# The end of a long convolution rewritten: tables closed two ticks sooner, a w_in block in a kernel tile's free half, the last units in a written order

## The chip, the cores and the metric

The program runs on one core of one Trainium2 chip. Its time is the device time of one execution in microseconds (us). Before and after are compared by the median of their runs. The engines are PE (TensorE matmul, with PEld for its weight loads), DVE (VectorE), ACT (ScalarE), POOL (GpSimd) and SP (SyncE, which here only issues DMAs).

## The reference

Two halves follow each other on a [2048, 576] activation. The first is a long convolution per channel (an S4 layer), whose kernel K is a sum of 128 complex exponentials; the second is a gated MLP with a spatial product over time.

```
h = layernorm(x) * (1 + ca) + sa
K = einsum("dn,dnl,dn->dl", C, exp(dt * A * l), dt * B).real       # 576 channels, 2048 taps
x = x + ga * (irfft(rfft(h) * rfft(K)) + h * Dskip)
h = layernorm(x) * (1 + cb) + sb
z = gelu(h @ w_in)                                                 # w_in [576, 4608]
z1, z2 = z[:, :2304], layernorm(z[:, 2304:])
x = x + gb * ((z1 * (w_sp @ z2 + b_sp)) @ w_out)
```

## The kernel before

`ssm` is the first half. It makes the taps from tables (exp, sin and cos on ScalarE, products on VectorE) in 36 groups `g` of 16 channels, and the convolution from small transforms on PE. All of it runs in *ticks* of one loop: in tick t the tables of group t are made, `kg_unit` multiplies those of group t-3, `k1_unit` transforms group t-4 and writes it into a k1 tile. The channels fall into five blocks `c` (four of 128, the last, `NC - 1`, of 64). For each block, units `i` follow: `u_load` and `u_unit` bring in and transform the input, `z_unit` multiplies it with the k1 tile, `v_unit` transforms back and writes rows to the DRAM tensor `v_d`. Then four y units `(c, q)`, each of four row tiles, read `v_d` back transposed (`y_vload`, two DMAs), add x (`y_xload`) and write `x1_d`. A dictionary `plan` holds the tick of each. A unit of 128 channels is written (c, q) below with c from 0, so (2, 0) to (4, 3) are the last twelve y units.

In the tick loop a scheduler may reorder the instructions. After the loop, `mlp.nc = mlp.tied` records the rest in program order on each engine (the helper's line 132 then stands for all of them in the profile), so what stands first in the code is issued first on its queue. That holds for the code after the loop and for `phase_a`.

SyncE issues the loads in its order. A DMA waits on its queue for the release of its buffer, for the data in DRAM that it reads, and for the landing of the DMA issued eight before it. POOL issues the writes in the same way.

The tables stand in a pool `tb`; `tabs.close()` gives its space to the second half: `mc`, `wzp` (with `wz`, the split w_in), `xz` and `stg` with two staging tiles `wst`. The second half of w_in (the z2 columns) comes in five blocks q of 512 columns (the last of 256). Each goes through four steps: `start_load` (three DMAs, 1.125 MB), `start_sum` (a sum of squares on ScalarE), `win_scale` (a product with ones on PE, then a power of two by small VectorE operations), `start_hi` (the fp16 high part, ScalarE) and `start_lo` (the low part and the last 64 rows, VectorE). Blocks 0 and 1 are loaded in ticks 20 and 24. Blocks 2 and 3 are loaded into `stg` after the loop, and block 4 in `phase_a`.

`phase_a` makes z2 for 16 row tiles `b`: statistics, `roots` and `ln2_rows` on VectorE, `turn` (five transposes on PE), the nt tile (high half by ScalarE in `turn_hi`, low half by VectorE in `turn_lo`), then five blocks of 14 matmuls `z2_mm(b, h)` against w_in block h, with a gelu each. A sum or scale recorded between two `z2_mm` stands between them on PE. `phase_b` is the spatial product and the output, and the change does not touch it.

PE's results of the convolution go through four PSUM buffers (`ps1`). The pools `xb`, `za`, `zb` and `v` have two buffers, `ue` and `us` four, `u1` five.

Of the kernel before, what the change touches and what calls it, by code (L numbers as in the profile page):

```python
# [144 lines left out]
def ssm(tc, I, x1_d, consts_s, dram, mod_d, mlp):  # L145
# [5 lines left out]
    with ExitStack() as ctx:  # L151
# [272 lines left out]
        def kg_unit(g):  # L424
# [8 lines left out]
            kk = kab[g] = tb.tile([128, 4, 64], F32, name="kab")  # L433
# [6 lines left out]
        def k1_unit(g):  # L440
            c, gi = divmod(g, 8)
            if gi == 0:
                k1t[c] = kp.tile([128, 32, 128], F32, name="k1")
            kk = kab.pop(g)
# [72 lines left out]
        def y_vload(c, q):  # L517
# [9 lines left out]
            if c == NC - 2 and q < 2:  # L527
                vt = [part("za"), part("zb")]
            else:
                vt = [part("u1", 5)[:, :4 * w] for _ in range(2)]  # L530
# [77 lines left out]
        for tick in range(NG + 4):  # L608
# [60 lines left out]
        tabs.close()  # L669
        mlp.nc = mlp.tied  # L670
        V, A, G, T, S = mlp.nc.vector, mlp.nc.scalar, mlp.nc.gpsimd, mlp.nc.tensor, mlp.nc.sync
        c3, c4 = NC - 2, NC - 1
        y_vload(2, 2)
        mlp.start()
        mlp.start_load(2)
        y_xload(2, 2)
        mlp.start_x1()
        for i in range(2):
            z_unit(c4, i)
            v_unit(c3, 6 + i)  # L680
        mlp.start_sum(0)
        for i in range(2):
            z_unit(c4, 2 + i)
            v_unit(c4, i)
            mlp.win_scale(5 + i, False)
            if i == 0:
                mlp.start_sum(1)
        mlp.start_hi(0)
        v_unit(c4, 2)
        v_unit(c4, 3)  # L690
        for c, r in ((2, 3), (c3, 0), (c3, 1), (c3, 2), (c3, 3), (c4, 0), (c4, 1), (c4, 2), (c4, 3)):
            y_xload(c, r)
        mlp.start_hi(1)
        mlp.start_lo(0)
        y_unit(2, 1)
        for c, r in ((2, 3), (c3, 0), (c3, 1), (c4, 0), (c4, 1)):
            y_vload(c, r)
        mlp.start_sums(ps2(), ps2())
        mlp.start_lo(1)
        y_unit(2, 2)  # L700
        y_vload(c3, 2)
        mlp.start_rows()
        mlp.start_sum(2)
        y_unit(2, 3)
# [57 lines left out]
class Mlp:  # L762
# [46 lines left out]
    def win_scale(self, q, inv=True):  # L809
        V, wcol = self.nc.vector, self.wcol  # L810
        self.total(wcol(q, N_W), q, 1)
# [4 lines left out]
    def win_last(self, q, t, dst):  # L816

        s = self.wcol(q, S_W)
        self.hi(dst[:, 8], t[:, 4], s)
        self.lo(dst[:64, 9], t[:64, 4], s[:64], dst[:64, 8])  # L820
# [65 lines left out]

    def start_sum(self, q):
# [730 lines left out]
```

## Time and profile before

| | us |
|---|---|
| median of 3 runs | 1798.19 (1791.86 to 1798.38) |
| profiled execution | 1798.62 |
| its span on the core | 1796.9 |
| PE busy | 1695.7 (94%) |
| DVE busy | 1128.8 (63%) |
| ACT busy | 785.6 (44%) |
| POOL busy | 224.0 (12%) |

The tick loop fills the first 400 us or so, `phase_a` runs from about 444 to 693, `phase_b` to the end. In the tables of windows each row has the busy time of the engines in a stretch, with the number of instructions, then the clock granted to PE, the mean share of time in which the 16 DMA engines worked (above 1 where transfers overlap on one engine), and GB/s. In timelines an entry has its start, its duration, engine, line, operation, tiles and shape, and in brackets the idle time of the engine ahead of it with what released it. SPq is SyncE's queue: the row is the issue of a DMA.

### The profile page before, as it was taken

How to read it: one execution, taken by the hardware profiler on the slowest of the kernel's cores; microseconds unless marked ns; L12 is line 12 of the kernel's file. 1: busy time of each engine (PE TensorE's matmuls, PEld its weight loads, DVE VectorE, ACT ScalarE, POOL GpSimd, SP SyncE). 2: the span in 40 equal slices, each digit the busy share in tenths (PEclk: the TensorE clock that was granted, in tenths of full speed). 3: DMA queues.
4: the chain of work that ended last, by engine and by line, in shares of the span. 5: the costliest groups of instructions: out<-in, count | busy, mean ns of one | idle time of the engine just before them, and what ended most of it. 6: DMA issues, size and time to landing. Idle time of an engine off the chain costs nothing.

```text
span 1796.9 us, 34078 instructions
## 1 busy us (share of the span) xinstructions
PE 1695.7 (94%) x14202; PEld 1197.6 (67%) x14202; DVE 1128.8 (63%) x2253; ACT 785.6 (44%) x1021; POOL 224.0 (12%) x350
## 2 busy tenths in 40 slices
PE   4687999996899999999999999999999999999999
PEld 1344555565455545877787777877778777887787
DVE  6987999857888997999784444474222265222322
ACT  4658999844476666555441322241111132011110
POOL 1321232342122211000000000000000000000000
PEclk8788999998899999999999999999999999999999
DMA  8457445779588788877564675562655472555520
GB/s 274 139 196 243 139 119 163 195 207 314 169 266 261 241 259 246 301 277 257 206 216 148 240 250 206 212 250 92 227 192 197 173 264 69 176 181 175 199 83 27
DMA packets 153034, 361.57 MB, mean 201 GB/s; under 512 B 24832, under 2 KB 68224, under 8 KB 150960
## 3 DMA queue, kind: packets, MB, share of 16 engines
q1 hardware_dynamic: 110272, 167.30, 29.4%
q0 software_dynamic: 33120, 153.95, 25.8%
q10 hardware_dynamic: 9488, 38.16, 5.3%
q8 instruction: 111, 1.82, 0.4%
q14 instruction: 43, 0.35, 0.1%
HBM read 256.86 MB, written 93.05 MB: 195 GB/s over the span
## 4 chain that ended last, share of the span: by engine, by line
PE 51%; DVE 16%; DMA 7%; issue 4%; ACT 4%; SPq 0%; POOL 0%; ACTq 0%; DVEq 0%; POOLq 0%
PE ps L1324 9%; PE ps L1359 8%; PE ps L1361 8%; PE ps L1360 8%; PE pz L132 3%; PE ps L1408 3%; PE ps L1409 3%; PE ps L1410 3%; DMA raw<-in_w_spT 2%; DVE zset L1066 2%; DVE gt L1373 2%; DMA z_d<-z 2%; ACT z L132 1%; DVE bsz L132 1%; PE pk L132 1%
## 5 line engine op out<-in xcount | busy, mean ns | idle before, releaser
L1359 PE MATMUL ps<-wsp,zset 128*128 128x256 f16 x2016 | 549.5, 273 | 2.8 <-DVE gt L1373 2.6
L1361 PE MATMUL ps<-wsp,zset 128*128 128x256 f16 x2016 | 549.5, 273 | 0.2 <-DVE zset L1066 0.2
L1360 PE MATMUL ps<-wsp,zset 128*128 128x256 f16 x2016 | 549.5, 273 | 0.0
L132 PE MATMUL pz<-wz,nt 128*128 128x512 f16 (+1 forms) x1120 | 227.2, 363 | 9.0 <-ACT nt L132 5.5
L1373 DVE SCALAR_TENSOR_TENSOR gt<-ps,sc,bsp 128x512 f32<-128x512 f32 x36 | 27.0, 749 | 316.1 <-PE ps L1361 316.1
L1324 PE MATMUL ps<-n2q,wf 128*128 128x512 f16 x1008 | 223.3, 379 | 0.6 <-DMA wf<-win_d 0.6
L1359 PEld LDWEIGHTS <-zset 128*128 128x128 f16 x2016 | 197.5, 98 | 29.7 <-DVE gt L1373 3.2
L1360 PEld LDWEIGHTS <-zset 128*128 128x128 f16 x2016 | 197.2, 98 | 26.1
L1361 PEld LDWEIGHTS <-zset 128*128 128x128 f16 x2016 | 197.3, 98 | 23.3 <-DVE zset L1066 0.5
L132 PEld LDWEIGHTS <-nt 128*128 128x128 f16 x1120 | 110.2, 100 | 117.4 <-ACT nt L132 7.2
L1324 PEld LDWEIGHTS <-wf 128*128 128x128 f16 x1008 | 98.6, 98 | 112.6 <-DMA wf<-win_d 1.1
L1336 POOL DMA_DIRECT2D zset<-set_d x96 | 51.1, 532 | 969.3 <-PE ps L1361 939.3
L1329 ACT ACTIVATE z<-ps,sc 128x512 f32<-128x512 f32 x56 | 37.8, 681 | 280.5 <-PE ps L1324 278.0
L1409 PE MATMUL ps<-wout,z 128*128 128x288 f16 x448 | 128.1, 286 | 0.0
L1408 PE MATMUL ps<-wout,z 128*128 128x288 f16 x448 | 128.1, 286 | 0.0
L1410 PE MATMUL ps<-wout,z 128*128 128x288 f16 x448 | 128.1, 286 | 0.0
L1373 DVE SCALAR_TENSOR_TENSOR gt<-ps,sc,gt 128x512 f32<-128x512 f32 (+1 forms) x180 | 121.9, 694 | 5.8 <-DVE gt L1373 0.5
L1066 DVE TENSOR_TENSOR zset<-raw,zset 128x1024 f16<-128x1024 f32 x48 | 58.6, 1220 | 74.7 <-ACT zset L1065 74.7
L1065 ACT ACTIVATE zset<-raw 128x1024 f16<-128x1024 f32 x48 | 50.3, 1051 | 97.5 <-PE ps L1361 70.1
L132 ACT ACTIVATE z<-pz,sc 128x512 f32<-128x512 f32 (+1 forms) x80 | 49.6, 646 | 56.8 <-DMA z_d<-z 44.4
L1418 DVE TENSOR_TENSOR ot<-ot,ps 128x288 f32<-128x288 f32 x32 | 14.2, 452 | 82.7 <-ACT ot L1417 82.7
L369 PE MATMUL ps<-ln_x,r1t 128*128 128x288 f32 x128 | 43.6, 499 | 19.0 <-issue 12.6
(311 smaller groups left out, 2827.5 us busy)
## 6 DMA issues: line engine op xcount, KB each, us to landing
zset<-set_d POOLq DMA_DIRECT2D x96, 896.0 KB, 4.9
set_d<-zset ACTq DMA_DIRECT2D x36, 896.0 KB, 5.8
raw<-z_d SPq DMA_DIRECT2D x48, 512.0 KB, 4.6
wf<-win_d SPq DMA_DIRECT2D x72, 320.0 KB, 3.4
raw<-in_w_spT SPq DMA_DIRECT2D x43, 512.0 KB, 6.0
z_d<-z POOLq DMA_DIRECT2D x32, 576.0 KB, 7.8
u_d<-st1o POOLq DMA_DIRECT2D x16, 576.0 KB, 4.5
u<-u_d SPq DMA_DIRECT2D x36, 256.0 KB, 4.8
```

What stands on the lines that cost most here:

```text
L132: return self.tc.keep_in_program_order(f(*a, **k))
L1065: nc.scalar.activation(o[:, k, 0], t, AF.Copy)
L1066: nc.vector.tensor_tensor(o[:, k, 1], t, o[:, k, 0], op=ALU.subtract)
L1324: nc.tensor.matmul(pm.rearrange("p (t c) -> p t c", t=4), w[:, kw], self.n2[q][:, :, kn], start=i == 0, stop=i == len(Z1) - 1)
L1336: self.nc.gpsimd.dma_start(o, self.set_d[n // 4, n % 4])
L1359: T.matmul(pm, z[:, a, 0, c], w[:, b, 0], start=i + half == 0, stop=False, skip_group_check=True)
L1360: T.matmul(pm, z[:, a, 0, c], w[:, b, 1], start=False, stop=False, skip_group_check=True)
L1361: T.matmul(pm, z[:, a, 1, c], w[:, b, 0], start=False, stop=i == 7, skip_group_check=True)
L1373: V.scalar_tensor_tensor(dst, pm, inv, to, op0=ALU.mult, op1=ALU.add)
L1408: T.matmul(pl, p[:, 1, ts], w[:, 0, hs], start=st, stop=sp)
L1409: T.matmul(pa, p[:, 0, ts], w[:, 0, hs], start=st, stop=False)
L1410: T.matmul(pa, p[:, 0, ts], w[:, 1, hs], start=False, stop=sp)
```

## The change

Seven things change together.

1. The tick loop ends two ticks sooner (`NG + 2`). What it would have recorded in ticks 38 and 39 is now written out after it, in program order, and between these units stand the first steps of the second half. `tabs.close()` comes after `kg_unit(NG - 1)` and `k1_unit(NG - 2)`, and the last group's `kab` tile lies in an `xb` buffer.
2. Block 2 of w_in is loaded in the tick loop into the half of the last k1 tile that 64 channels leave free (`load_two`, 1 MB), its last 64 rows later into a `u1` buffer (`load_last`). Its sum of squares is two instructions, added by one reduction (`sum_two`, `total(..., 20, 2)`).
3. `stg` takes blocks 3 and 4, so that `start_load(3)` stands ahead of most y loads, and `start_load(4)` behind them but ahead of `phase_a`.
4. The low parts of blocks 0 and 1 are written in two pieces each among the z and v units (`start_lo(q, 0)` and `start_lo(q, 1)`; the second is `last`, the two operations that `win_last` had).
5. Y unit (2, 1) stands between the v units of the last block; units (3, 0), (2, 2) and (4, 0) come first after them, then the normed rows of tile 0, then the other eight.
6. Sum, scale, high and low part of block 2, and sum, scale and high part of block 3 are ahead of `phase_a`. There `start_lo(3)` stands behind `turn_lo(0)`, and block 4's four steps around the first gelu.
7. Y load (2, 3) takes the `za` and `zb` buffers that (3, 0) had; (3, 0) takes `u1`.

The core of the diff:

```diff
-            kk = kab[g] = tb.tile([128, 4, 64], F32, name="kab")
+            if g < NG - 1:
+                kk = kab[g] = tb.tile([128, 4, 64], F32, name="kab")
+            else:
+                kk = kab[g] = part("xb")[:, :256].rearrange("p (i w) -> p i w", i=4)
...
+                if c == NC - 1:
+                    t = k1t[c].rearrange("p a b -> p (a b)")
+                    k1t[c] = t[:, :32 * CHL].rearrange("p (a b) -> p a b", b=CHL)
+                    mlp.load_two(2, t[:, 32 * CHL:].rearrange("p (k n) -> p k n", k=4))
...
-            if c == NC - 2 and q < 2:
+            if (c, q) in ((NC - 2, 1), (NC - 3, 3)):
                 vt = [part("za"), part("zb")]
...
-        for tick in range(NG + 4):
+        for tick in range(NG + 2):
...
-        tabs.close()
         mlp.nc = mlp.tied
         V, A, G, T, S = mlp.nc.vector, mlp.nc.scalar, mlp.nc.gpsimd, mlp.nc.tensor, mlp.nc.sync
-        c3, c4 = NC - 2, NC - 1
-        y_vload(2, 2)
+        c2, c3, c4 = NC - 3, NC - 2, NC - 1
+        y_load(c2, 0)
+        u_load(c4, 2)
+        u_load(c4, 3)
+        z_unit(c3, 4)
+        z_unit(c3, 5)
+        v_unit(c3, 2)
+        v_unit(c3, 3)
+        kg_unit(NG - 1)
+        d_unit(NG - 1)
+        u_unit(c4, 0)
+        u_unit(c4, 1)
+        k1_unit(NG - 2)
+        tabs.close()
         mlp.start()
-        mlp.start_load(2)
-        y_xload(2, 2)
+        mlp.start_sum(0)
+        z_unit(c3, 6)
+        z_unit(c3, 7)
+        y_vload(c2, 1)
+        y_xload(c2, 1)
+        v_unit(c3, 4)
+        v_unit(c3, 5)
+        mlp.win_scale(5, False)
+        mlp.start_hi(0)
+        u_unit(c4, 2)
+        u_unit(c4, 3)
+        k1_unit(NG - 1)
+        y_unit(c2, 0)
+        mlp.load_last(2, part("u1", 5))
+        mlp.start_load(3)
         mlp.start_x1()
-        for i in range(2):
-            z_unit(c4, i)
-            v_unit(c3, 6 + i)
-        mlp.start_sum(0)
-        for i in range(2):
-            z_unit(c4, 2 + i)
-            v_unit(c4, i)
-            mlp.win_scale(5 + i, False)
-            if i == 0:
-                mlp.start_sum(1)
-        mlp.start_hi(0)
+        y_xload(c3, 0)
+        y_xload(c4, 0)
+        z_unit(c4, 0)
+        mlp.start_sum(1)
+        mlp.start_lo(0, 0)
+        v_unit(c3, 6)
+        z_unit(c4, 1)
+        mlp.start_lo(0, 1)
+        mlp.win_scale(6, False)
+        v_unit(c3, 7)
+        y_vload(c3, 0)
+        z_unit(c4, 2)
+        mlp.start_hi(1)
+        v_unit(c4, 0)
+        mlp.start_lo(1, 0)
+        z_unit(c4, 3)
+        y_unit(c2, 1)
+        v_unit(c4, 1)
+        mlp.start_sums(ps2(), ps2())
         v_unit(c4, 2)
+        mlp.start_lo(1, 1)
         v_unit(c4, 3)
-        for c, r in ((2, 3), (c3, 0), (c3, 1), (c3, 2), (c3, 3), (c4, 0), (c4, 1), (c4, 2), (c4, 3)):
+        mlp.sum_two(2)
+        y_vload(c2, 2)
+        for c, r in ((c2, 2), (c2, 3), (c3, 1), (c3, 2), (c3, 3), (c4, 1), (c4, 2), (c4, 3)):
             y_xload(c, r)
-        mlp.start_hi(1)
-        mlp.start_lo(0)
-        y_unit(2, 1)
-        for c, r in ((2, 3), (c3, 0), (c3, 1), (c4, 0), (c4, 1)):
-            y_vload(c, r)
-        mlp.start_sums(ps2(), ps2())
-        mlp.start_lo(1)
-        y_unit(2, 2)
+        y_vload(c4, 0)
+        y_vload(c2, 3)
+        y_vload(c3, 1)
+        y_vload(c4, 1)
+        mlp.start_rows()
+        y_unit(c3, 0)
+        mlp.win_scale(7)
+        mlp.start_hi(2)
+        y_unit(c2, 2)
+        mlp.start_sum(3)
+        mlp.start_lo(2)
         y_vload(c3, 2)
-        mlp.start_rows()
-        mlp.start_sum(2)
-        y_unit(2, 3)
-        y_vload(c3, 3)
         y_vload(c4, 2)
-        y_vload(c4, 3)
-        mlp.start_load(3)
-        mlp.win_scale(7)
-        y_unit(c3, 0)
         y_unit(c4, 0)
-        mlp.start_hi(2)
         mlp.ap = mlp.wzp
         mlp.ln2_stats(0)
-        y_unit(c3, 1)
+        y_vload(c3, 3)
+        y_vload(c4, 3)
+        mlp.start_load(4)
         mlp.roots(x=0)
-        y_unit(c4, 1)
         mlp.ln2_rows(0)
+        for c, r in ((c2, 3), (c3, 1), (c4, 1)):
+            y_unit(c, r)
+        mlp.win_scale(8)
+        mlp.start_hi(3)
         for c, r in ((c3, 2), (c4, 2), (c3, 3), (c4, 3)):
             y_unit(c, r)
         mlp.nc = tc.nc
...
+    def load_two(self, q, t):
+        self.wts[q] = [t, None]
+        self.nc.sync.dma_start(t, self.I["w_in"][:512, FH + 512 * q:FH + 512 * q + 512].rearrange("(k p) n -> p k n", p=128))
+    def load_last(self, q, t):
+        self.wts[q][1] = t
+        for h in range(2):
+            self.nc.sync.dma_start(t[64 * h:64 * h + 64], self.I["w_in"][512:, FH + 512 * q:FH + 512 * q + 512])
+    def sum_two(self, q):
+        A, (t, u) = self.nc.scalar, self.wts[q]
+        for i, (x, w) in enumerate(((t, self.wz[:, 0:4, 512 * q:512 * q + 512]), (u, self.wz[:, 4, 512 * q:512 * q + 512]))):
+            A.activation(w, x, AF.Square, accum_out=self.acc[:, 20 + i:21 + i])
+    def main_last(self, q, n):
+        t = self.wts[q]
+        return t if isinstance(t, list) else (t[:, 0:4, :n], t[:, 4, :n])
     def start_sum(self, q):
         n = min(512, FH - 512 * q)
         self.win_sum(5 + q, self.wts[q], self.wz[:, 0:5, 512 * q:512 * q + n], n)
     def start_hi(self, q):
         n = min(512, FH - 512 * q)
-        self.hi(self.wz[:, 0:4, 512 * q:512 * q + n], self.wts[q][:, 0:4, :n], self.wcol(5 + q, S_W), act=True)
-
-    def start_lo(self, q):
+        self.hi(self.wz[:, 0:4, 512 * q:512 * q + n], self.main_last(q, n)[0], self.wcol(5 + q, S_W), act=True)
+    def start_lo(self, q, *parts):
         n = min(512, FH - 512 * q)
-        t, w = self.wts.pop(q)[:, :, :n], self.wz[:, :, 512 * q:512 * q + n]
-        self.lo(w[:, 4:8], t[:, 0:4], self.wcol(5 + q, S_W), w[:, 0:4])
-        self.win_last(5 + q, t, w)
+        (t, u), w, s = self.main_last(q, n), self.wz[:, :, 512 * q:512 * q + n], self.wcol(5 + q, S_W)
+        for part in parts or (0, 1):
+            if part == 0:
+                self.lo(w[:, 4:8], t, s, w[:, 0:4])
+            else:
+                self.last(u, w, s)
...
             if b == 0:
                 self.turn(0)
                 self.turn_hi(0)
-                self.start_lo(2)
-                self.start_load(4)
                 self.x1_load(4)
                 self.turn_lo(0)
+                self.start_lo(3)
         self.ln2_stats(2)
         for b in range(16):
             do(b, LD)
             self.z2_mm(b, 0)
             do(b, A0)
             if b == 0:
-                self.start_sum(3)
-                self.win_scale(8)
+                self.start_sum(4)
+                self.win_scale(9)
             self.z2_gelu(b, 0)
             if b == 0:
-                self.start_hi(3)
-                self.start_lo(3)
+                self.start_hi(4)
+                self.start_lo(4)
...
-            if b == 0:
-                self.start_sum(4)
-                self.win_scale(9)
-                self.start_hi(4)
...
-            if b == 0:
-                self.start_lo(4)
```

What stands on SyncE's queue at the end of the convolution, before: u1 tiles are y loads of block 2, ident to xz the start loads, wst_4315 is w_in block 2, us_4437 the x rows of a y unit.

```order
L533 DMA u1_4215<-v_d_84 128x4x128
L132 DMA u1_4286<-v_d_84 128x4x128
L132 DMA ident_4295<-in_c_small 128x128
L132 DMA u1_4287<-v_d_84 128x4x128
L132 DMA mrow_4301<-mod_d_66 128x1152
L132 DMA x1l_4305<-in_x 128x12x64
L132 DMA xz_4310<-in_x 128x4x192
L132 DMA wst_4315<-in_w_in 128x4x512
L132 DMA wst_4315<-in_w_in 64x512 x2
L132 DMA xb_4319<-in_x 128x4x128
L132 DMA xz_4310<-x1_d_60 128x4x384
L132 DMA us_4437<-in_x 128x4x128
```

And now (wst_4329 is w_in block 3, u1_4326 the last rows of block 2, u1_4260 and u1_4261 y load (2, 1), u1_4388 the first half of y load (3, 0)):

```order
L132 DMA x1l_4231<-in_x 128x12x64
L132 DMA xz_4236<-in_x 128x4x192
L132 DMA u1_4260<-v_d_84 128x4x128
L132 DMA u1_4261<-v_d_84 128x4x128
L132 DMA xb_4264<-in_x 128x4x128
L132 DMA u1_4326<-in_w_in 64x512 x2
L132 DMA wst_4329<-in_w_in 128x4x512
L132 DMA wst_4329<-in_w_in 64x512 x2
L132 DMA xz_4236<-x1_d_60 128x4x384
L132 DMA u1_4388<-v_d_85 128x4x128
L132 DMA u1_4389<-v_d_85 128x4x128
```

The start loads stand ahead of y load (2, 1), block 3 has the place of block 2, and y load (3, 0) the place right behind the load of x1.

What stands on VectorE at the start of `phase_a`, before: the last y unit's add, wso's memset, the low part of w_in block 2 (wst_4315), nt's low half of tile 0, the statistics of tile 1.

```order
L132 TENSOR_TENSOR x1l_4305<-pk_4658,x1l_4305 128x256
L132 MEMSET wso_4690 64x4x64
L132 SCALAR_TENSOR_TENSOR wz_4303<-wst_4315,sc_4297,wz_4303 128x4x512
L132 TENSOR_SCALAR wz_4303<-wst_4315,sc_4297 128x512
L132 SCALAR_TENSOR_TENSOR wz_4303<-wst_4315,sc_4297,wz_4303 64x512
L132 TENSOR_TENSOR nt_4698<-pt_4692,nt_4698 128x512
L132 TENSOR_TENSOR nt_4698<-pt_4692,nt_4698 64x128
L132 BN_STATS bsx_4713<-xz_4310 128x6 x2
```

And now, where wst_4329 is block 3:

```order
L132 TENSOR_TENSOR x1l_4231<-pk_4683,x1l_4231 128x256
L132 MEMSET wso_4715 64x4x64
L132 TENSOR_TENSOR nt_4723<-pt_4717,nt_4723 128x512
L132 TENSOR_TENSOR nt_4723<-pt_4717,nt_4723 64x128
L132 SCALAR_TENSOR_TENSOR wz_4229<-wst_4329,sc_4223,wz_4229 128x4x512
L132 TENSOR_SCALAR wz_4229<-wst_4329,sc_4223 128x512
L132 SCALAR_TENSOR_TENSOR wz_4229<-wst_4329,sc_4223,wz_4229 64x512
L132 BN_STATS bsx_4734<-xz_4236 128x6 x2
```

Nt's low half has moved ahead of a block's low part.

On ScalarE at the same place, before: sum and high part of block 2 (wst_4315), nt's high half, then block 3 (wst_4538) and block 4 (wst_4704) among the first gelus (z2).

```order
L132 ACTIVATE wz_4303,acc_67<-wst_4315 128x5x512
L132 ACTIVATE wz_4303<-wst_4315,sc_4297 128x4x512
L132 ACTIVATE nt_4698<-pt_4692 128x512
L132 ACTIVATE nt_4698<-pt_4692 128x128
L132 ACTIVATE wz_4303,acc_67<-wst_4538 128x5x512
L132 ACTIVATE z2_4776<-pz_4747,sc_4297 128x512
L132 ACTIVATE wz_4303<-wst_4538,sc_4297 128x4x512
L132 ACTIVATE z2_4776<-pz_4803,sc_4297 128x512
L132 ACTIVATE wz_4303,acc_67<-wst_4704 128x5x256
L132 ACTIVATE wz_4303<-wst_4704,sc_4297 128x4x256
```

And now, where k1_3991 and u1_4326 hold block 2, wst_4329 block 3 and wst_4579 block 4:

```order
L132 ACTIVATE wz_4229,acc_67<-k1_3991 128x4x512
L132 ACTIVATE wz_4229,acc_67<-u1_4326 128x512
L132 ACT_TABLE_LOAD
L132 ACTIVATE sc_4223<-ones_4219 128x1
L132 ACTIVATE wz_4229<-k1_3991,sc_4223 128x4x512
L132 ACTIVATE wz_4229,acc_67<-wst_4329 128x5x512
L132 ACTIVATE wz_4229<-wst_4329,sc_4223 128x4x512
L132 ACTIVATE nt_4723<-pt_4717 128x512
L132 ACTIVATE nt_4723<-pt_4717 128x128
L132 ACTIVATE wz_4229,acc_67<-wst_4579 128x5x256
L132 ACTIVATE z2_4797<-pz_4768,sc_4223 128x512
L132 ACTIVATE wz_4229<-wst_4579,sc_4223 128x4x256
```

Block 3's sum and high part have moved ahead of nt, and block 4's sum ahead of the first gelu.

More of the change, by code (lines that the diff above doesn't have):

```diff
@@ L810, in win_scale @@
         V, wcol = self.nc.vector, self.wcol
-        self.total(wcol(q, N_W), q, 1)
+        self.total(wcol(q, N_W), *((20, 2) if q == 7 else (q, 1)))
         pow2_scale(V, self.mc, wcol(q, N_W), wcol(q, S_W), wcol(q, I_W))
@@ L816, in win_last, with last @@
     def win_last(self, q, t, dst):
-        s = self.wcol(q, S_W)
-        self.hi(dst[:, 8], t[:, 4], s)
-        self.lo(dst[:64, 9], t[:64, 4], s[:64], dst[:64, 8])
+        self.last(t[:, 4], dst, self.wcol(q, S_W))
+    def last(self, u, dst, s):
+        self.hi(dst[:, 8], u, s)
+        self.lo(dst[:64, 9], u[:64], s[:64], dst[:64, 8])
     def sums(self, c0, n):
```

## The prediction

> **What bounds the kernel now.** First the page: the span, and PE's busy tenths in 40 slices of 44.9 us. Then the table by windows around the two weak slices (404 to 494 us): here the columns are busy us of PE, PEld, DVE, ACT, POOL, the granted clock, the DMA share and GB/s.
>
> ```profile
> span 1796.9 us, 34078 instructions
> ...
> PE   4687999996899999999999999999999999999999
> ```
>
> ```profile
> 390.00:400.00 10.00, 10.00 (x77) 6.56 (x76) 3.38 (x5) 3.58 (x6) 4.82 (x10) 1.00 0.77 195
> ...
> 410.00:420.00 10.00, 10.00 (x67) 6.37 (x65) 7.28 (x21) 7.96 (x10) 2.17 (x4) 1.00 1.07 327
> 420.00:430.00 10.00, 2.48 (x22) 1.86 (x18) 8.77 (x21) 5.03 (x7) 1.52 (x2) 0.62 1.13 342
> 430.00:440.00 10.00, 7.49 (x86) 6.59 (x85) 7.56 (x31) 2.87 (x3) 3.15 (x5) 0.70 1.12 287
> 440.00:450.00 10.00, 6.50 (x65) 4.02 (x66) 9.15 (x16) 3.19 (x4) 4.16 (x6) 0.98 0.90 287
> 450.00:460.00 10.00, 5.47 (x22) 2.59 (x21) 7.59 (x29) 4.20 (x4) 0.00 (x1) 0.84 0.30 102
> 460.00:470.00 10.00, 9.63 (x33) 4.10 (x34) 9.20 (x32) 2.73 (x7) 0.00 (x0) 0.66 0.69 227
> 470.00:480.00 10.00, 10.00 (x58) 5.51 (x56) 9.25 (x29) 4.79 (x6) 0.56 (x1) 1.00 0.60 198
> ```
>
> PE is full up to 420 and again from 461. Between them it is idle for 40 - (2.48 + 7.49 + 6.50 + 5.47) = 18.1 us, and the clock is low. That is all that an edit of this seam can win: PE is the limit on both sides, so what the first z2 blocks gain is carried to the end. The timeline of PE names the waits.
>
> ```profile
> 418.29 1.97 PE L132 MATMUL pk<-u,st 128*64 128x128 f32 x32
> 427.09 0.66 PE L132 MATMUL pk<-u,st 128*64 128x128 f32 x2 [6.84 <-DMA u<-v_d]
> ...
> 444.75 1.90 PE L132 MATMUL pz<-wz,nt 128*128 128x512 f16 x8 [0.69 <-ACT nt L132]
> 448.63 1.77 PE L132 MATMUL pz<-wz,nt 128*128 128x512 f16 x6 [1.98 <-DVE nt L132]
> ...
> 450.48 4.45 PE L132 MATMUL pz<-wz,nt 128*128 128x512 f16 x14
> 454.76 0.71 PE L132 MATMUL pt<-ident,n 128*128 128x128 f32 x5
> 460.37 0.58 PE L132 MATMUL pz<-acc,ones 128*128 128x1 f32 x2 [4.90 <-ACT wz L132]
> 460.82 13.66 PE L132 MATMUL pz<-wz,nt 128*128 128x512 f16 x56
> ```
>
> Three waits hold most of it: 6.84 us for the reloaded v rows, then 1.98 us because the w_in low part stands ahead of nt's low part on VectorE, then 4.90 us because block 4's sum stands on ScalarE behind block 3's high part and a gelu. The 56 matmuls that end at 474.48 are my mark: three blocks of z2 tile 0 and one of tile 1; PE is full behind them.
>
> What paces the y units is SyncE's queue. From the timeline, the chain and the table of DMA issues:
>
> ```profile
> 427.16 3.66 SPq L132 DMA_DIRECT2D ue<-v_d  x4
> ...
> 434.15 3.30 SPq L132 DMA_DIRECT2D ue<-v_d  x4
> ```
>
> ```profile
> 436.79 5.85 DMA ue<-v_d
> ```
>
> ```profile
> v_d<-v POOLq DMA_DIRECT2D x12, 256.0 KB, 3.9
> ...
> ue<-v_d SPq DMA_DIRECT2D x8, 128.0 KB, 5.0
> ...
> v_d<-ue POOLq DMA_DIRECT2D x2, 256.0 KB, 6.4
> ```
>
> The last 12 loads go out at (437.45 - 427.16) / 12 = 0.86 us each, with the DMA share above 1, and the last lands at 442.64.
>
> **The change, part by part.** Durations of VectorE and ScalarE come from these rows of the timeline (start to start where a row follows directly):
>
> ```profile
> 417.76 2.35 DVE L132 SCALAR_TENSOR_TENSOR wz<-wst,sc,wz 128x2048 f16<-128x2048 f32 x1 [0.95 <-ACT wz L132]
> ...
> 421.21 0.68 DVE L132 TENSOR_TENSOR xb<-pk,xb 128x512 f32<-128x512 f32 x1
> ...
> 448.93 0.82 DVE L132 BATCH_NORM_STATS2 bsx<-xz 128x6 f32<-128x288 f32 x2
> ...
> 450.03 0.15 DVE L132 TENSOR_SCALAR vh<-mvx 128x1 f32<-128x1 f32 x1
> ...
> 452.41 0.81 DVE L132 SCALAR_TENSOR_TENSOR n<-xz,mvx,mrow 128x576 f32<-128x576 f32 x1
> ...
> 454.22 0.81 DVE L132 BATCH_NORM_STATS2 bsx<-xz 128x6 f32<-128x288 f32 x2
> ...
> 455.30 0.16 DVE L132 COPY sc<-pz 128x1 f32<-128x1 f32 x1
> ...
> 470.63 1.00 DVE L132 TENSOR_TENSOR nt<-pt,nt 128x512 f16<-128x512 f32 x2
> ```
>
> ```profile
> 418.39 0.60 ACT L132 ACTIVATE ue<-pk 128x512 f32<-128x512 f32 x1 [0.18 <-PE pk L132]
> ...
> 428.45 2.32 ACT L132 ACTIVATE wz<-wst 128x2560 f16<-128x2560 f32 x1
> ...
> 432.74 2.00 ACT L132 ACTIVATE wz<-wst,sc 128x2048 f16<-128x2048 f32 x1 [1.87 <-DVE sc L132]
> 444.09 0.77 ACT L132 ACTIVATE nt<-pt 128x512 f16<-128x512 f32 x2 [9.35 <-PE pt L132]
> 456.49 2.00 ACT L132 ACTIVATE wz<-wst,sc 128x2048 f16<-128x2048 f32 x1 [5.37 <-DVE sc L132]
> ```
>
> So a low part with its two last pieces is 421.21 - 417.76 = 3.45 us, statistics 1.10, a root 2.38, the normed rows 1.81, nt's low part 1.00, and from a scale's copy to the high part that uses it 1.19.
>
> *The last two ticks in written order.* PE's order is the same but for one thing: y unit (2,1) now stands ahead of the last three v units, so the last v unit ends half of the 1.97 us row later, at 418.29 + 0.98 = 419.3. ScalarE gets two sums and two high parts among the evictions; it is busy 3.58 of 10 us at 390 to 400, so I put this at nothing. Its price, if PE's four PSUM buffers do not cover it, is a rival below.
>
> *Block 2's megabyte* goes into the free half of the last k1 tile, on SyncE's queue behind y load (1,3)'s first half, near 358; at 342 GB/s (row at 420) it takes 3.1 us. Nothing waits for it before block 2's sum, and behind it on the queue stand the other half of that y load and u loads for units of later ticks: I take nothing, at worst 3.1. Its old place is taken by block 3, so the bytes of the full stretch stay; the start loads (ident, mrow, x1l, xz) go out earlier, ahead of the last k1 unit. The kab tile in an xb buffer waits for that buffer's write on ScalarE, off the path: nothing.
>
> *SyncE's new order.* The y loads now wait three times: start_x1 for y (2,0)'s write, y load (3,0) for v unit (3,7), and y load (4,0) for the last v unit; all other loads of rows 1 to 3 are queued behind that last wait. The write goes out at 420.1. It lands 3.9 to 6.4 us later (the two rows of v_d), the load 5.0 after: 429.1 to 431.5. VectorE wants it at 430.1 (next part), less 0.5 for the y unit, so the slip is 0 to 1.9 us; I take 0.6, near the low end, as the queue has had time to drain. [...]
>
> *The chain to the first z2 block.* Last v unit 419.3, eviction 0.60, block 2's sum in two pieces (2.32 for one; 2.3 to 3.1, I take 2.7): 422.6. To the high part 1.87 and a reduction of 0.2: 424.7; high part 2.00: 426.7; low part 3.45: 430.1. Now y (4,0)'s add 0.4, statistics, root and rows 5.29: row tile 0 at 435.8. Three adds 1.6 and a scale 1.19: block 3's high part from 438.6 to 440.6, which is now ahead of nt: nt's high half 441.4. So the first z2 block starts at 441.4 instead of 444.75, by 3.4 us.
>
> *The first z2 blocks.* Nt's low part comes first now, 442.4: the 1.98 us wait is gone. Behind it on VectorE stands block 3's low part, 445.9, then statistics, root and rows, 5.29: tile 1 can be turned at 451.2, before at 454.76. PE has two blocks of 14 until then, at most 4.45 each: 441.4 + 8.9 + 0.5 = 450.8, hidden. Block 4's sum needs no gelu ahead any more, so the 4.90 us wait is gone. After the turn (0.6) come the same 56 matmuls: at 13.66 us they end at 465.5. That is 474.48 - 465.5 = 9.0 us. At the full clock they take 10.76:
>
> ```profile
> 580.02 10.76 PE L132 MATMUL pz<-wz,nt 128*128 128x512 f16 x56
> ```
>
> Then they would end at 462.6, but nt 1's low part holds the last six: VectorE took 471.6 - 454.22 = 17.4 us from there before, and loses block 3's low part (3.45), a scale (1.2) and the wait for that high part (about 1.5): 11.3, so 462.5 and 1.2 of matmuls: 463.7, a gain of 10.8. Which of the two it is hangs on the clock, and about that the windows show this:
>
> ```profile
> 446.25:449.66 3.41, 1.43 (x7) 0.51 (x6) 3.31 (x7) 2.40 (x2) 0.91 (x2) 1.00 0.68 175
> 449.67:453.07 3.40, 3.40 (x11) 1.56 (x10) 2.92 (x16) 0.70 (x2) 0.33 (x1) 0.50 0.96 321
> ```
>
> A stretch in which PE was busy 1.43 of 3.41 us was followed by half the clock, while 440 to 450, with 6.50 of 10 busy, kept 0.98. In my chain PE is idle about 0.5 us ahead of the turn, so I take 10.4, near the full clock's end. The Trainium skill (TensorE: Matmul & The Clock Gate, Why this matters for your kernels) asks only that no idle gap exceeds some 3 us. By that rule even the 2 us gap would have kept the clock and the gain is the 10.8, with the halved clock of the 13.66 us row 9.0; the two rows differ from the rule, and they decide.
>
> **The sum.** 10.4 - 0.6 = 9.8 us. The profiled execution took 1798.62 us (its span 1796.9 and 1.7 around it), 0.4 above the median of 1798.19. 1798.6 - 9.8 = 1788.8.
>
> **Rivals.** *Late loads.* Everything for rows 1 to 3 that is queued behind the last v write leaves only then: 14 loads from about 426.5, at the old pace of 0.86 us until 438.5, the last landing 5.85 later at 444.4. The turn of tile 0 is due at 439.9 (nt's high half at 440.6, less the 0.71) and comes 5.0 later; the gain is 10.4 - 5.0 = 5.4: 1793.2. For it: the DMA share above 1 from 420 to 440. Against it: 3.1 MB at 342 GB/s are 9.0 us, and the queue has been empty ahead of them.
>
> *ScalarE holds PE up* before 419: four pieces (two sums, two high parts) of 2.32 and 2.00 stand among evictions, up to 8.6 us if none of it is covered: about 1797.5, no change. Against it: four PSUM buffers, and ScalarE's 3.58 of 10 us.
>
> *Slower: SyncE's queue.* Y load (3,0) waits until 415, and nine loads go out behind it at 0.86 until 423. The last v write stands in their backlog, 6.4 + 5.85 from 420.1: 432.4. Then 16 loads at 0.86 end at 446.1 and land at 452. The turn comes at 452.5, 12.6 after its due time, and 10.4 - 12.6 = -2.2: 1800.8. It is slower from the point at which the last load lands after 450. For it: the same share above 1; against it: what stands on the queue until 407 is issued earlier than before, and that empties it. Its tail (the row loads of z2 late as well) reaches 1810.
>
> **Chances.** Forecast 0.64 (own range 1786.0 to 1791.5), late loads 0.20, ScalarE 0.07, SyncE's queue 0.09. The least that a measurement can tell is 0.5%, 9.0 us: 1789.2 and 1807.2. Some six tenths of the forecast are faster by that much and 0.02 of late loads; the rest of these and ScalarE are within; of SyncE's queue somewhat more than half is slower: 0.41, 0.54, 0.05. The range of 1785.0 to 1796.5 leaves out ScalarE, SyncE's queue and 0.03 below.
>
> **What would show it.** Right: the last v unit near 419.3, row tile 0 near 436, the first z2 matmul near 441.4 (a wait on ScalarE's nt), the turn of tile 1 near 451 with VectorE as releaser, no wait of PE on block 4's sum. Wrong: PE idle before 415, a last y load that lands after 441, or PE waiting for VectorE again after 470, since it is busy 9.25 of 10 there and has little to give.

## The result, and the profile after

The changed kernel took 1787.91 us (median of 6 runs, 1783.43 to 1790.96) against 1798.13 (6 runs, 1791.86 to 1800.51): ratio 0.9946, 95% interval 0.9925 to 0.9967. Run once more beside 29 runs of before it gave 0.9964 (0.9952 to 0.9977). The forecast was 1788.8. The number came out; the sum behind it did not quite, and that is the subject of what follows. In the tables and labels below, *before* and *after* are the kernel without and with the change.

First PE's timeline of after over *the seam*, the stretch between the last v unit and the place from which PE is full again in `phase_a`:

```profile
415.68 0.40 PE L132 MATMUL pk<-u,st 128*64 128x128 f32 x2 [0.30 <-DMA u<-v_d]
...
426.18 1.57 PE L132 MATMUL pk<-ue,st 128*64 128x64 f32 x16 [6.01 <-DMA ue<-v_d]
...
437.06 0.98 PE L132 MATMUL pk<-u,st 128*64 128x128 f32 x13 [0.86 <-DMA u<-v_d]
...
440.00 3.20 PE L132 MATMUL pz<-wz,nt 128*128 128x512 f16 x14 [0.69 <-ACT nt L132]
443.03 0.28 PE L132 MATMUL pz<-acc,ones 128*128 128x1 f32 x2
443.17 3.18 PE L132 MATMUL pz<-wz,nt 128*128 128x512 f16 x14
449.93 1.30 PE L132 MATMUL pt<-ident,n 128*128 128x128 f32 x5 [3.57 <-DVE n L132]
451.02 13.00 PE L132 MATMUL pz<-wz,nt 128*128 128x512 f16 x56
```

The waits of 1.98 and 4.90 us are gone. In their place PE is idle for 6.01 us ahead of y unit (4, 0) and for 3.57 us ahead of row tile 1's turn. The 56 matmuls end at 464.02 instead of 474.48: 10.46 us, against 9.8 forecast. But look at a row that stands well ahead of the changed code, ScalarE's table load in the last kernel tile, and at the gelu of row tile 1's first block (timelines of ScalarE, before and then after):

```profile
347.30 1.28 ACT L386 ACT_TABLE_LOAD   x1
...
474.56 0.69 ACT L132 ACTIVATE z<-pz,sc 128x512 f32<-128x512 f32 x1 [0.28 <-issue]
```

```profile
343.20 1.28 ACT L386 ACT_TABLE_LOAD   x1
...
464.10 0.69 ACT L132 ACTIVATE z<-pz,sc 128x512 f32<-128x512 f32 x1 [0.28 <-issue]
```

4.1 of the 10.46 us were there before the change began. I call the time from that table load's start to that gelu's end *the stretch*: 475.25 - 347.30 = 127.95 before, 464.79 - 343.20 = 121.59 after. The seam gains 6.4 us. As the two traces are 4.1 us apart already there, what is compared between traces below is counted from that table load.

VectorE's share of it stands in its windows, after first and then before, from the table load to 72.2 us behind it, where after's last v unit ends (columns as in the prediction):

```profile
343.20:390.00 46.80, 45.28 (x569) 28.76 (x567) 29.92 (x50) 28.52 (x39) 16.20 (x27) 1.00 0.85 227
390.00:415.38 25.38, 25.38 (x150) 16.24 (x148) 19.98 (x40) 12.65 (x17) 7.81 (x14) 1.00 1.06 296
```

```profile
347.30:394.10 46.80, 45.29 (x569) 28.76 (x567) 29.78 (x49) 26.44 (x37) 14.58 (x26) 1.00 0.82 207
394.10:419.48 25.38, 25.37 (x156) 16.51 (x156) 13.78 (x32) 12.88 (x16) 8.92 (x14) 1.00 0.94 282
```

In the first 46.8 us VectorE does the same in both. In the 25.4 us behind them it works 19.98 us instead of 13.78, beside a PE that is full: 6.2 us of work that stood in the seam before, above all low parts of w_in.

### The profile page after: what moved, and what is told of

Same layout as the page of the kernel before. It is cut to its first block, busy times and chain, and to the rows that moved or that the text cites. A ratio compares the mean times of both kernels' runs of the same rounds, so it can differ in the third digit from the quotient of the medians.

```text
span 1789.2 us, 34076 instructions
## 1 busy us (share of the span) xinstructions
PE 1698.4 (95%) x14202; PEld 1197.6 (67%) x14202; DVE 1128.4 (63%) x2254; ACT 785.6 (44%) x1023; POOL 224.3 (13%) x350
## 4 chain that ended last, share of the span: by engine, by line
PE 46%; DVE 16%; DMA 9%; issue 8%; ACT 3%; POOL 1%; SPq 0%; ACTq 0%; DVEq 0%; POOLq 0%
PE ps L1383 8%; PE ps L1418 8%; PE ps L1419 8%; PE ps L1420 8%; DVE zset L1132 3%; PE pz L132 3%; PE ps L1467 2%; PE ps L1468 2%; PE ps L1469 2%; DVE gt L1432 2%; DMA raw<-in_w_spT 2%; DMA z_d<-z 2%; DVE bsz L132 1%; ACT z L132 1%; DMA gbs<-in_w_out 1%
## 5 line engine op out<-in xcount | busy, mean ns | idle before, releaser
L1477 DVE TENSOR_TENSOR ot<-ot,ps 128x288 f32<-128x288 f32 x32 | 14.2, 452 | 82.7 <-ACT ot L1476 82.7
```

## The experiments

My theory (V) was by now: the seam is as long as VectorE's chain, from row tile 0's normed rows to nt's low part of tile 1; PE's waits are its shadow. The rivals: PE's own waits are the loss (W), or the loads set the time (late loads). Ahead of these stands the question whether the first 343 us differ by chance (A) or by the change (B). The table has four marks of each trace, from the timelines. "Rows", "turn 1" and "stretch" are us from the table load's start: the end of row tile 0's rows, the start of tile 1's turn, the end of that gelu.

| kernel | table load | rows | turn 1 | stretch | ratio to before (95%) |
|---|---|---|---|---|---|
| before | 347.30 | 94.07 | 107.47 | 127.95 | |
| before_again | 342.88 | 94.03 | 107.44 | 128.25 | 1.0013 (0.9993 to 1.0033) |
| lo_behind | 345.43 | 93.92 | 109.35 | 130.16 | 1.0008 (0.9995 to 1.0021) |
| scale_later | 343.54 | 93.84 | 107.24 | 129.14 | 1.0022 (0.9999 to 1.0045) |
| after | 343.20 | 90.28 | 106.72 | 121.59 | 0.9946 (0.9925 to 0.9967) |
| again | 342.83 | 89.82 | 106.73 | 121.56 | 0.9964 (0.9952 to 0.9977) |
| lo_ahead | 340.24 | 89.88 | 106.83 | 120.35 | 0.9959 (0.9944 to 0.9974) |
| clock_fill | 342.04 | 90.59 | 106.97 | 120.50 | 0.9960 (0.9938 to 0.9982) |
| v_split | 342.43 | 91.20 | 107.63 | 121.42 | 0.9949 (0.9929 to 0.9969) |
| loads_first | 341.82 | 93.80 | 110.29 | 123.82 | 0.9982 (0.9963 to 1.0000) |
| seam_pad | 346.53 | 90.17 | 109.53 | 123.50 | 0.9969 (0.9953 to 0.9985) |
| block_back | 340.63 | 90.36 | 105.42 | 126.26 | 0.9973 (0.9953 to 0.9994) |
| best | 346.10 | 90.36 | 104.24 | 117.76 | 0.9950 (0.9934 to 0.9966) |

**Both kernels again.**

> The changed kernel once more, nothing edited. The two traces so far differ already ahead of the changed code: the ScalarE table load of the last kernel tile starts at 347.30 before and 343.20 after, 4.1 us earlier. From there to the gelu of row tile 1's first block (ends 475.25 and 464.79) it is 127.9 us before and 121.6 after, 6.4 less; from there to the end of the span after takes 2.8 us more. Theory A (the seam alone): the first 343 us differ by chance, the seam does not. The table load then starts anywhere from 340 to 350, the stretch of 121.6 comes out within 1 us, and the gain of the whole, about 10 us in the median, is 6.4 of the seam and the rest what lies behind it. Theory B (the change moves the start as well): the table load comes again within 1 us of 343.2.

> The kernel of before once more, nothing edited, for a second trace of it and as the measure of what no edit can do: ratio 1.000 within 0.002. Theory A: its table load of the last kernel tile (347.30 in the first trace) moves by some us, while the stretch from there to the gelu of row tile 1's first block stays 127.9 within 1 us. Theory B: the table load comes within 1 us of 347.3.

Theory A holds in the main. The table load comes anywhere from 340.24 to 347.30 in the thirteen traces, whose kernels have the same work ahead of it, while the stretch repeats to 0.03 us in after and 0.3 in before. With this scatter a small shift cannot be excluded: the table load comes at 344.8 in the mean of the four kernels built on before and at 342.9 in the nine built on after. What follows the stretch varies as well: 1321.7 and 1325.7 us to the span's end in the two traces of before, 1324.4 and 1321.0 in those of after. So a total is good to some us only, and the stretch tells tenths. The second comparison, 0.36% of 1797 or 6.5 us, is the seam's 6.4, and a gain of 6.4 us lies in the interval of the first one too.

**The order on VectorE.** lo_ahead puts one line of the change back, lo_behind does that one edit in before:

```diff
# lo_ahead: in after
+                self.start_lo(3)
                 self.x1_load(4)
                 self.turn_lo(0)
-                self.start_lo(3)
# lo_behind: in before
-                self.start_lo(2)
                 self.start_load(4)
                 self.x1_load(4)
                 self.turn_lo(0)
+                self.start_lo(2)
```

> The changed kernel with one line put back: w_in block 3's low part stands again ahead of nt's low part of row tile 0 on VectorE. Theory A: the first z2 block loses its last six matmuls to a wait of about 3.45 us less 1.9, some 1.5 to 2 us; but behind it VectorE does the same work in the same time, so tile 1's turn comes at the same distance from the first z2 block (9.9 us within 0.5) and the gelu of row tile 1's first block within 1 us: the time is that of the changed kernel within 0.2%. Rival: the order is where the gain is (1.98 us of wait that the trace of before shows): the stretch to that gelu grows by 2 us or more.

> The kernel of before with one edit of the change alone: the third w_in block's low part behind nt's low part of row tile 0 on VectorE, all else as before. Theory A: the 1.98 us wait in the first z2 block goes, but VectorE comes no earlier to tile 1's normed rows, so the wait of 4.90 stays or grows and the stretch from the last kernel tile's table load to the gelu of row tile 1's first block stays 127.9 within 0.7 us: same time as before. Rival: 1.98 us are gained.

The rival is out: taking the 1.98 us wait away gains nothing. In lo_ahead the first z2 block starts 1.35 us later after the table load than in after (98.15 instead of 96.80), and yet VectorE ends nt's low part of tile 1 at 118.4, as in after (118.3). The new order is even a small loss, 1.2 us of stretch in after (the clock's, as clock_fill below shows) and about 2 in before, where I had expected a change of at most 0.7. Part of the latter is seen on VectorE in lo_behind, which now waits for nt's high half while the low part stands behind it:

```profile
444.99 1.02 DVE L132 TENSOR_TENSOR nt<-pt,nt 128x512 f16<-128x512 f32 x2 [1.16 <-ACT nt L132]
```

In before that low part filled this time. Against what I had expected, lo_ahead's first z2 block shows no wait; it ran at the low clock instead (14 matmuls in 5.08 us), where it cost nothing, and the clock was back for the 56.

**PE's wait for block 4's sum.** The 4.90 us wait was on a matmul of 128x1, queued ahead of blocks that had all they needed:

```diff
             if b == 0:
+                self.z2_mm(b, 2)
+                self.z2_mm(b, 3)
                 self.start_sum(4)
                 self.win_scale(9)
...
-            self.z2_mm(b, 2)
+            if b > 0:
+                self.z2_mm(b, 2)
...
-            self.z2_mm(b, 3)
+            if b > 0:
+                self.z2_mm(b, 3)
```

> The kernel of before with one edit: PE computes row tile 0's third and fourth z2 block ahead of the small matmul that totals w_in block 4, the one that waited 4.90 us for ScalarE. All else, VectorE's order too, as before. Stretch: from the ScalarE table load of the last kernel tile to the end of the gelu of row tile 1's first block, 127.95 and 128.25 us in two traces of before, 121.6 in two of after. Theory W (PE's waits are the loss): PE gets the 4.90 us back, the stretch is about 123 and the time 4.9 us less than before. Theory V (VectorE's chain sets the end, the wait of PE is its shadow): nt's low part of row tile 1, which ended 124.3 us after that table load, stays there within 0.5, PE waits for it instead, and the stretch is 126.6 to 128.4, the time that of before.

The stretch was 1 us longer than in before, 0.7 beyond V's range. PE, then one row of VectorE, timelines of scale_later:

```profile
450.77 0.71 PE L132 MATMUL pt<-ident,n 128*128 128x128 f32 x5
451.32 4.27 PE L132 MATMUL pz<-wz,nt 128*128 128x512 f16 x18
456.95 2.32 PE L132 MATMUL pz<-wz,nt 128*128 128x512 f16 x10 [1.36 <-DVE wz L132]
459.11 0.28 PE L132 MATMUL pz<-acc,ones 128*128 128x1 f32 x2
464.56 1.01 PE L132 MATMUL pz<-wz,nt 128*128 128x256 f16 x4 [5.17 <-ACT wz L132]
466.00 5.90 PE L132 MATMUL pz<-wz,nt 128*128 128x256 f16 x24 [0.43 <-DVE wz L132]
```

```profile
466.65 1.00 DVE L132 TENSOR_TENSOR nt<-pt,nt 128x512 f16<-128x512 f32 x2
```

PE starts the third z2 block 107.8 us after the table load instead of 113.5 and waits 1.36 + 5.17 + 0.43 for the parts of blocks 3 and 4 instead. Nt's low part of tile 1 ends at 467.65, 124.1 after the table load; in before 124.3. W is out: the wait was VectorE's shadow. The last matmuls of block 4 then ran at half the clock (granted 0.50 from 465.94 to 469.35; 24 of them took 5.90 us, against 4.27 in lo_behind), which is enough for the extra time. V does not hold to the last microsecond in before: from the end of nt's low part to the end of the gelu it is 3.6 us there, but 2.0 in lo_ahead, where PE waits for VectorE. So up to 1.6 us of before's stretch are PE's, at a granted clock of 0.66 (row at 460 in the prediction).

**VectorE's work itself.** seam_pad adds 2.35 us to the chain:

```diff
                 self.turn_lo(0)
                 self.start_lo(3)
+                self.start_lo(3, 0)
```

> The changed kernel with VectorE doing the 128x2048 piece of w_in block 3's low part twice (2.35 us more, same values), behind nt's low part of row tile 0. Theory V: row tile 1's turn comes 2.35 later (109.1 after the table load instead of 106.7) and the stretch to row tile 1's first gelu is 122.9 (VectorE's end of 120.5 plus 2.35) to 123.9 (the turn plus the 14.9 us that followed it in after, at the low clock), against 121.6. If VectorE had slack there, 121.6 again.

The turn came at 109.53 and the stretch was 123.50: V, the turn 0.4 us later than forecast. block_back undoes the blocks' part of the change:

```diff
# ssm: mlp.win_scale(8) and mlp.start_hi(3) taken out; phase_a:
-                self.start_lo(3)
...
             if b == 0:
-                self.start_sum(4)
-                self.win_scale(9)
+                self.win_scale(8)
             self.z2_gelu(b, 0)
             if b == 0:
-                self.start_hi(4)
-                self.start_lo(4)
+                self.start_hi(3)
+                self.start_lo(3)
... behind z2_gelu(b, 1):
+            if b == 0:
+                self.start_sum(4)
+                self.win_scale(9)
+                self.start_hi(4)
... behind turn_hi(b + 1):
+            if b == 0:
+                self.start_lo(4)
```

> The changed kernel with the steps of w_in blocks 3 and 4 put back where the last two blocks stood before: block 3's scale, high and low part around the first gelu, block 4's sum, scale and high part behind the second, its low part ahead of nt's. The tail ahead of phase_a stays as changed but for block 3's scale and high part. Theory V by VectorE's rows: row tile 1's turn comes about 103.3 us after the last kernel tile's table load (106.7 in after), since nothing of block 3 is ahead of it; behind it follow statistics, scale 1.5, a wait of 1.5 for ScalarE, low part 3.45, root and rows 4.2, scale 1.5, high part 1.2, low part 2.1, nt 1.0: nt's low part of tile 1 ends near 121.5 (118.3 in after) and the stretch is 123.3 to 124.7. Then 3.3 to 4.7 of the 6.4 us are the tail's (row tile 0's rows 3.8 us sooner) and the rest is the blocks' steps. Rival: the blocks' steps are all of it, 127.5 to 128.5; or nothing of it, 121.6.

126.26 lies between the forecasts: a miss by 1.6 us. The wait on block 4's sum came back, with 5.42 us, and nt's low part of tile 1 ended at 122.85. In this trace the first z2 block also came late (98.94 after the table load, 96.80 in after): the matmuls of the last y load that PE waited for started at 94.7 instead of 93.9, and the turn ran at the low clock (1.33 us instead of 0.77). The edit does not touch these loads, but that it has no part in this is not shown. So of the 6.4 us the blocks' steps hold 2.5 to 4.7, depending on whether those 2.1 are counted, and the tail 1.7 to 3.8; one trace does not settle it closer. The traces of before and after, read directly, divide the 6.4 us so: row tile 0's rows end 3.8 us sooner (90.28 instead of 94.07), from there to the end of nt's low part of tile 1 it is 28.0 us instead of 30.3, and the rest 0.3. No run puts back the low parts that now stand beside the full PE, so what they alone bring is read from the windows and not tested.

**The loads.** v_split lets the last v writes send y load (4, 0)'s part first; loads_first moves four loads ahead of the one that waits:

```diff
# v_split
-            G.dma_start(v_d[c][:, kr(c, i)], by(v, c))
+            if c == NC - 1 and i > 1:
+                G.dma_start(v_d[c][:32, kr(c, i)], by(v[:32], c))
+                G.dma_start(v_d[c][32:, kr(c, i)], by(v[32:], c))
+            else:
+                G.dma_start(v_d[c][:, kr(c, i)], by(v, c))
# loads_first
-        y_vload(c4, 0)
         y_vload(c2, 3)
         y_vload(c3, 1)
+        y_vload(c4, 0)
         y_vload(c4, 1)
```

> The changed kernel, but the last two v units write their rows in two DMAs each, the 32 partitions that y load (4,0) reads (64 KB) first, the other 96 (192 KB) behind. In after the last write took 6.4 us, the load 3.3, and VectorE stood idle from 425.93 to 427.78 ahead of y unit (4,0)'s add, 1.85 us. Theory R (this round trip, no longer VectorE, sets row tile 0's rows in after): the small write lands about 2 us sooner, the rows (90.28 and 89.82 us after the table load) come 1 to 1.85 sooner, and the stretch to row tile 1's first gelu falls from 121.6 by up to 1.2, to the 120.4 at which VectorE ended it in the run with the low part ahead. Theory V0 (my prediction: VectorE sets it there too): the rows come within 0.3 of where they were. Either way the time is that of after within 0.2%.

> The changed kernel with SyncE's order altered in one place: the four loads of y (2,3) and (3,1), whose rows are long written, are issued ahead of y load (4,0), which waits for the last v write, instead of behind it. Late-loads theory: the last y load lands about 4 x 0.5 = 2.0 us sooner, row tile 0's turn (95.35 us after the table load in both traces of after) comes 1.2 sooner, the first z2 block with it, and VectorE's 0.66 us wait in the adds goes. Theory V: the turn of tile 0 moves so, but row tile 1's turn (106.72) moves by at most 0.7, the wait of VectorE that goes, and the stretch to row tile 1's first gelu (121.6) by no more. Against both: y (4,0)'s load behind four more issues comes up to 1.5 later, and the rows with it.

Neither helped. The small write of v_split was hardly faster: the load that waits for it went out 421.72 - 415.52 = 6.2 us after the write, in after 422.76 - 416.31 = 6.45. PE's idle time ahead of y unit (4, 0) fell from 6.01 to 3.91 us, but the loads of y (3, 0) landed later and shifted VectorE's chain; the rows came 0.9 to 1.4 later. In loads_first the idle time grew (PE, then SyncE's queue):

```profile
428.36 1.41 PE L132 MATMUL pk<-ue,st 128*64 128x64 f32 x15 [9.58 <-DMA ue<-v_d]
```

```profile
422.62 3.83 SPq L132 DMA_DIRECT2D ue<-v_d  x4
```

From issue to matmul it is 428.36 - 422.62 = 5.7 us; in after, with SyncE's queue idle ahead of it, 426.18 - 422.76 = 3.4. The issue itself came 1.2 us later after the table load. The rows came 3.5 us later and the stretch was 2.2 longer. The wait on the queue that I had priced as a risk had drained it, and that was worth more than the four earlier loads.

The loads are not off the path in after, though. Its chain of waits runs to tile 0's nt through the last y loads, and only from there on along VectorE:

```profile
431.62 5.40 DMA u<-v_d
437.06 1.55 PE pk L132 x28
438.62 0.71 PE pt L132 x5
439.35 0.78 ACT nt L132 x2
440.15 0.69 DVE nt L132
```

The second trace of after agrees: its rows come 0.46 us sooner (89.82), yet the turn of tile 0 (95.36, in after 95.35) and that of tile 1 do not. VectorE waits 0.66 + 0.55 us in this piece, so V holds strictly only from nt of tile 0 on.

**The clock.** clock_fill gives PE 14 matmuls of nt and wz to do in the 3.57 us, into a PSUM tile of their own (`fill`, a helper not shown):

```diff
             self.z2_mm(b, 1)
+            if b == 0:
+                self.fill(14)
             if b + 1 < 16:
                 self.turn(b + 1)
```

> The changed kernel with 14 matmuls more, whose result nobody reads, on PE between row tile 0's second z2 block and the turn of row tile 1, where PE stood idle for 3.57 us in after and then ran at half the clock (turn 1.30 instead of 0.71, the 56 matmuls 13.00). Clock theory: the idle time is the cause; filled with some 3.2 us of matmuls, the clock stays at 1.00, the turn takes 0.71 and the 56 matmuls 9.5 to 11.9. By theory V VectorE then ends the stretch, nt's low part at 461.5 in the old times: 120.4 instead of 121.6, and PE shows a wait of about 1 us for it. If PE alone set the time there, it would be 119.2. If the idle time is not the cause, 13.0 and 121.6 again.

```profile
442.71 6.20 PE L132 MATMUL pz<-wz,nt 128*128 128x512 f16 x28
449.01 0.74 PE L132 MATMUL pt<-ident,n 128*128 128x128 f32 x5
449.58 9.46 PE L132 MATMUL pz<-wz,nt 128*128 128x512 f16 x50
460.30 1.47 PE L132 MATMUL pz<-wz,nt 128*128 128x512 f16 x6 [1.25 <-DVE nt L132]
```

As forecast: full clock, the last six matmuls wait for VectorE, 120.50. In after itself the low clock, not VectorE, held the last 1.1 us.

**A kernel that gains more.** best takes block 3 out of VectorE's chain:

```diff
+        mlp.win_scale(8)
+        mlp.start_hi(3)
         y_vload(c3, 2)
         y_vload(c4, 2)
         y_unit(c4, 0)
...
-        mlp.win_scale(8)
-        mlp.start_hi(3)
-        for c, r in ((c3, 2), (c4, 2), (c3, 3), (c4, 3)):
+        for c, r in ((c3, 2), (c4, 2)):
+            y_unit(c, r)
+        mlp.start_lo(3)
+        for c, r in ((c3, 3), (c4, 3)):
             y_unit(c, r)
... phase_a:
                 self.turn_lo(0)
-                self.start_lo(3)
```

> The changed kernel with w_in block 3 taken further out of VectorE's chain: its scale and ScalarE's high part ahead of y unit (4,0)'s add, where VectorE stood idle for 1.85 us in after, and its low part (3.45 us) ahead of the last two y adds, for which VectorE waited 0.66 us, instead of behind nt's low part. Theory V (VectorE's chain from row tile 0's rows to nt's low part of row tile 1 sets the end): the scale (1.5) and the waits (0.66 and 0.55) leave the chain, row tile 1's turn comes 103.5 to 104.5 after the last kernel tile's table load instead of 106.7, PE's idle time ahead of it falls from 3.57 to under 1.5 us, so the clock stays, and the stretch to row tile 1's first gelu is 117.5 to 119 instead of 121.6: about 3 us less than after, 9 to 10 less than before, ratio 0.9945 to 0.996. Rival (the last y load sets row tile 0's turn and all behind it): the stretch stays at 120.4 or more and the time is that of after.

```profile
447.04 3.18 PE L132 MATMUL pz<-wz,nt 128*128 128x512 f16 x14
450.34 0.74 PE L132 MATMUL pt<-ident,n 128*128 128x128 f32 x5
450.91 9.46 PE L132 MATMUL pz<-wz,nt 128*128 128x512 f16 x50
```

The stretch is 117.76, 3.8 us less than after and 10.2 less than before; PE goes from tile 0's second block to tile 1's turn without a wait. It took 1787.64 us, 0.9950 of before (0.9934 to 0.9966). By the trace it beats both; by the totals it beats before, and its interval still meets that of after.

## Why the prediction came out, and where it was wrong

All times below are counted from the table load (347.30 in the trace the prediction used, 343.20 in after).

- *Written order of the last ticks, block 2's megabyte: nothing.* Right. The last v unit was forecast at 419.3, 72.0 after the table load, and ended at 415.38, 72.2. PE was not idle ahead of it.
- *VectorE to the end of block 2's low part.* Right: 82.8 forecast, 425.93 or 82.7 measured.
- *SyncE's new order: 0.6 us.* The bound 0 to 1.9 held, the value did not: VectorE waited 1.85. The write took 6.40 us (chain of waits) and the load 3.4, so the data were there at 83.0, as the value of 0.6 asks (82.9). But from the start of the y unit to VectorE's add I had put 0.5 us, and it took 427.78 - 426.18 = 1.6: after 6.01 us of idle time PE ran at half the clock, and the 16 matmuls took 1.57 us instead of the 0.63 of a later y unit.

```profile
416.31 6.40 DMA v_d<-ue
...
435.06 0.63 PE L132 MATMUL pk<-ue,st 128*64 128x64 f32 x16
```

So the rows came at 90.3 (89.8 in again) instead of 89.1 with the slip.
- *First z2 block.* 94.7 was forecast with the slip, 96.8 measured. The adds waited 0.66 us for the last y loads and the turn stood behind them on PE. This is a part of the late-loads rival come true: PE waits for the last u load until 437.06, 93.9 after the table load or 441.2 in the times of the prediction, and so the last load landed past the 441 that it had named as a sign of being wrong, if well short of the rival's 444.4. None of my edits to the loads recovered it, so its size by itself was not shown.
- *Turn of tile 1, 9.8 us behind the first z2 block.* Right: 9.93, with VectorE as releaser. But I had put PE's two blocks at 4.45 us each, from a row at the low clock, and so saw 0.5 us of idle time ahead of the turn; they took 3.2 each and the idle time was 3.57.
- *The 56 matmuls near the full clock.* Wrong through that step: 13.00 us, near the other end that I had given.
- *Sum.* Forecast 9.8, the stretch shows 6.4: 3.4 too much, of which 2.1 stand at the first z2 block, 0.1 at the turn and 1.2 are the clock. How the 2.1 divide between the rows, 1.2 late, and the loads is not shown. The total met the forecast since the first comparison showed 10.2 us, in runs whose parts ahead of and behind the stretch vary by more than these 3.4 us. To that extent the agreement was luck.
- *Rivals.* ScalarE did not hold PE up, SyncE's queue did not fall behind, and PE did not wait for VectorE where 470 to 520 of the prediction's times lie.
- The prediction read the three waits as three losses. Only VectorE's chain behind them was one: the first two came back under other names (6.01 and 3.57 us), and taking the second or the third away alone gained nothing. A row of the prediction pointed there already: ScalarE's high part of block 3, behind which block 4's sum stands, had itself waited 5.37 us for VectorE's scale.

## What to carry to other kernels

Before pricing a wait of an in-order engine, look for the engine that is busy all through it (here VectorE, 7.6 to 9.2 of every 10 us from 420 to 470 in before): here removing a wait only moved it, and taking that engine's work out of its chain shortened the seam. When a change concerns 40 us of 1800, measure it from a row shortly ahead of it to one shortly behind; the rest of the trace can differ by more than the change, with no edit at all. Moving loads ahead of the one that the others wait for can cost more than it brings: in loads_first that load lost 1.2 us on the queue and 2.3 from issue to use.

## What the runs showed of the hardware

The same idle time of 3.57 us ahead of tile 1's turn cost differently by where it fell. In the clock records of the thirteen traces the half clock always lasts a whole number of windows of 3.41 us (one to five; the end of a trace aside), so the clock changes on a fixed grid. Windows of PE on this grid (busy, then the granted clock, DMA share and GB/s) in after, v_split and loads_first:

```profile
445.35:448.76 3.41, 1.01 (x5) 0.99 0.87 285
448.76:452.17 3.41, 2.24 (x8) 0.50 0.97 276
452.17:455.58 3.41, 3.41 (x9) 0.51 0.55 213
```

```profile
444.40:447.80 3.40, 2.09 (x10) 1.00 0.79 240
447.80:451.20 3.40, 1.14 (x8) 1.00 1.09 325
451.20:454.60 3.40, 3.40 (x10) 0.50 0.83 311
```

```profile
447.10:450.51 3.41, 1.44 (x7) 1.00 0.63 204
450.51:453.92 3.41, 1.81 (x11) 1.00 1.05 322
```

In after the clock was halved for two windows of 3.41 us, in v_split for one, in loads_first, where the idle time is spread over two windows, not at all. A window with PE busy 1.01 or 1.14 us was followed by half the clock, one with 2.09 was not; while halved, 2.24 busy us did not bring it back. Between them the busy time alone does not tell: 1.44 us kept the clock in loads_first, 1.43 in before (the window in the prediction) lost it. The Trainium skill (TensorE: Matmul & The Clock Gate, Why this matters for your kernels) warns of idle gaps above some 3 us; by these rows the length of a gap does not decide alone. That its place on the grid does is what the three traces suggest; no run moved the gap and nothing else.
